# A routed two-layer feed-forward kernel: the blank bucket rows written last in the set-up, and the count of surely full tiles rounded up

## Chip, cores and metric

The kernel runs on one core of one Trainium2 chip. The metric is the device time of one launch in microseconds. It includes everything between the kernel's start and its last write: loading the weights, the scan, the routing, the matrix products and the scatter of the results.

## The reference

Two stages follow each other. The first is a gated recurrence along the sequence, for 4 batches of 5056 positions with 256 channels each. The second sends each of the 20224 resulting rows to the one expert of 8 with the largest logit, and applies that expert's two weight matrices (256 to 1024 to 256).

```python
sig = 1.0 / (1.0 + np.exp(-f_logit))
f = lower_bound + (1.0 - lower_bound) * sig
for t in range(S):
    h = f[:, t] * h + (1.0 - f[:, t]) * x[:, t]
    y[:, t] = h
...
logits = x @ w_gate
expert_idx = np.argmax(logits, axis=1)
gate_w = softmax(logits)[np.arange(N), expert_idx]
for e in range(E):
    mask = expert_idx == e
    h = np.maximum(x[mask] @ w1[e], 0.0)
    out[mask] = gate_w[mask, None] * (h @ w2[e])
```

## The kernel before

**Units.** The 20224 rows are worked on as 79 units of 256 rows. For each unit SP issues two loads (`load`, lines 248 and 249), ScalarE computes the gate (`prep`), VectorE runs the recurrence (`scan`, lines 264 to 277), and `split` scales the result, writes it as two fp16 halves and has SP transpose them into rows (line 297). `logits` multiplies by the gate matrix on TensorE (line 304).

**Groups and buckets.** Units are collected into 25 groups: one of 4 units, ten of 2, then groups of 4 (the last has 3). When a group's last unit is done, `route` finds each row's expert, and `place` works out where the row goes in that expert's bucket in DRAM (`idx`, line 352) and scatters the rows from GpSimd, 128 rows per indirect DMA (line 363). Bucket rows start 128 rows behind the bucket's first address. The first 128 rows of each bucket are written by `blank` (lines 238 to 243): a zeroed tile `zr`, whose token column lies out of bounds, is copied by one DMA of 8 x 128 rows of 1032 bytes. `zr` is taken from the rotation of three buffers with the tag `xT`.

**Tiles.** A tile is a run of 128 rows (groups 0 to 12) or 256 rows (groups 13 to 24) of one expert. Which expert has a full tile is known only on the chip, but how many tiles are surely full is known when the program is written: `guaranteed(n, size)` (line 57) gives it from the number n of rows that lie in the buckets and are not yet in a tile. `tile_info` (lines 380 to 428) then finds on VectorE the offset and the expert of that many tiles, in ten small instructions (lines 398 to 419), and puts the tiles into the list `todo`. What is left at the end goes into `NTAIL` tail tiles of 128 rows (`tail_info`); the last three of them stand in a branch that runs only if there are so many.

**Steps.** `prefetch` takes a tile of 256 rows, or two of 128 rows if the next in `todo` is one too, and has SP load it (`fetch`, lines 487 to 490): a register load of the offset, a transposing load of the rows into an `xT` buffer, and a small load `me`. At most three are fetched ahead. A `step` multiplies one fetched piece by w1 (`gemm1`, lines 508 to 510, three products for each pair of fp16 halves, in four blocks), evicts each block with ScalarE and VectorE (lines 513 and 514), and multiplies the piece of the step before by w2 (`gemm2`, lines 542 to 544, then line 548 and the scatter of line 549).

**Order.** The set-up follows the hand-written string `ORDER`. `L` loads one expert's weight matrix, `X` one unit, `P` runs `prep`, `T` finishes a unit up to its logits, `A`, `B`, `C` scale and split weights, `F` is `finish` (place the groups that are routed, and their tiles), `Q` is `prefetch`, `S` is a first step that holds only gemm1, and `W` is `blank`. In the set-up a scheduler may pull instructions forward in each engine's queue, but each engine works its queue in order. Behind the set-up TensorE, ScalarE and VectorE follow the program's own order: each step calls `fill` eight times if its gemm2 works on two tiles (four times in gemm1, twice for each tile of gemm2), and the parts of the next units are hung on these slots. The parts of a unit lie at fixed slots from its start: split at 0, scan of the next unit at 1, logits at 4, `finish` at 9. The distance to the next unit's start depends on the rows that are ready (in `todo` or fetched):

```python
def ready():
    return sum(t for t, _ in todo) + sum(f[4] for f in fetched)
...
plan_unit(tick(u), 5 if r < LOW else 6 if r < MID else 7 if r < HIGH else 8)
```

LOW, MID and HIGH are 1024, 1280 and 1792 rows.

Of the kernel before, what the change touches and what calls it, by code (L numbers as in the profile page):

```python
# [17 lines left out]
P = 128  # L18
D = 256
E = 8  # L20
F = 1024
# [16 lines left out]
LOW = 4 * UNIT  # L38
MID = 5 * UNIT
HIGH = 7 * UNIT  # L40
ORDER = "Q L X P X T Z L X L A0 P L X X L A1 W T B0 P X L L L P C0 T B1 T F P X Q A2 C1 Q P L A3 B2 L B3 C2 C3 L X T X T L L L F Z X L A4 B4 A6 T P P A5 X T C4 L P B5 B6 C5 C6 F A7 B7 T S Q C7"
EXPM = 0x7F800000
EVEN = 0x7F000000
MAGIC = 12582912.0
# [11 lines left out]

def guaranteed(n, size):

    return max(0, (n - E * (size - 1)) // size)


@with_exitstack
def moe_kernel(ctx: ExitStack, tc: tile.TileContext, x, fl, lb, wg, w1, w2, cst, tok, out, xb, S):
# [158 lines left out]
    def free(d, *groups, keep=()):  # L222

        for k in groups:
            tc.declare_no_dep(d.ins, group=k, keep=[s.ins for s in keep], reason="different rows")
# [10 lines left out]
    def blank():  # L236

        zr = p2.tile([P, ROW], F32, tag="xT", name="zr", bufs=3)
        nc.vector.memset(zr, 0.0)
        nc.vector.memset(zr.bitcast(I32)[:, D + 1:D + 2], OOB)  # L240
        d = nc.sync.dma_start(xb[0:E * CAP, :].rearrange("(e r) w -> r e w", e=E)[0:P], zr.unsqueeze(1).to_broadcast([P, E, ROW]))
        free(d, "scatter")
        tc.add_to_no_dep_group("blank", d.ins)

    def load(u):
# [312 lines left out]
    plan, n, taken = [], 0, 0  # L558
    while n < NU:
        gu = min(GROUPS[len(plan)] if len(plan) < len(GROUPS) else GRU, NU - n)  # L560
        n += gu
        size = P if len(plan) < SMALL else UNIT
        k = guaranteed(n * UNIT - taken, size)
        taken += k * size
        plan.append((gu, size, k))
# [128 lines left out]
    u = 0  # L694
    for w in ORDER.split():
        k, n = w[0], int(w[1:] or 0)
        if k == "L" and wl:
            wload(*wl.pop(0))
        elif k == "X":
            ahead(len(loaded))  # L700
        elif k == "P":
            preps(prepped[0])
        elif k == "Z":
            scans(scanned[0])
        elif k == "T":
            scans(u)
            t1 = tick(u)
            t1[2]()
            t1[3]()
            u += 1  # L710
        elif k == "A":
            stages[n] = wscale(*jobs[n][:2])
            stages[n][0]()
        elif k == "B":
            stages[n][1]()
        elif k == "C":
            stages[n][2]()
            jobs[n][2]()
        elif k == "W":
            blank()  # L720
        elif k == "F":
            finish()
        elif k == "Q":
            prefetch()
        elif k == "S":
            step(lambda k: None, False)
# [58 lines left out]
    if spare:  # L785
        n = nc.values_load(total[0])
# [93 lines left out]
```

## Time and profile before

| what | value |
|---|---|
| device time, median of 3 runs | 1008.66 us (1008.51 to 1011.13) |
| device time of the profiled execution | 1012.38 us |
| span of the profiled execution, first to last instruction | 1010.6 us |
| TensorE busy with products | 944.3 us (93%) |
| VectorE busy | 662.0 us (66%) |
| ScalarE busy | 485.4 us (48%) |
| GpSimd busy | 341.0 us (34%) |
| mean DMA rate | 144 GB/s |

The profile shows one execution. Shares over the whole span are averages over stages that differ: in the set-up the weights are loaded and split, behind it steps and units are interleaved, and at the end only steps are left. Such a profile is read by stages: first where TensorE, the busiest engine, stands idle, then what ended each idle stretch.

### The profile page before, as it was taken

The page shows a single profiled execution, that of the slowest core. Times are in us where ns is not written, and L with a number is a line of the kernel's source. Part 1 is how long each engine was busy: PE and PEld are TensorE (multiplying, and loading weights), DVE is VectorE, ACT ScalarE, POOL GpSimd, SP SyncE. Part 2 cuts the span into 40 slices and gives each one's busy share as a digit, 9 for nine tenths or more (in the row PEclk, how much of TensorE's full clock was granted, in tenths as well). Part 3 has the DMA queues.
Part 4 walks back from the last instruction along what each step waited for, and adds up shares of the span by engine and source line. Part 5 has one row for each costly group of instructions (what it writes and reads, how often), then busy time and mean ns, then how long its engine had stood idle before and what let it go on. Part 6 is the DMA issues. An engine that isn't in the chain of part 4 may idle for free.

```text
span 1010.6 us, 29046 instructions
## 1 busy us (share of the span) xinstructions
PE 944.3 (93%) x10815; PEld 852.6 (84%) x10815; DVE 662.0 (66%) x1885; ACT 485.4 (48%) x860; POOL 341.0 (34%) x351
## 2 busy tenths in 40 slices
PE   3549888999999999899999999999999999999998
PEld 3426877889999998888888888888888888899997
DVE  6987878778678677867877777677676423223231
ACT  4568544545545555545555555545553333233332
POOL 0141144434334533534552452442434321111212
PEclk9969988999999999999999999999999999999999
DMA  8997567979866767777786676567753321222211
GB/s 292 333 343 187 108 141 151 161 164 177 143 157 163 155 144 165 173 169 160 180 175 157 164 162 152 148 137 170 166 111 95 80 49 48 58 49 49 42 40 41
DMA packets 239579, 145.52 MB, mean 144 GB/s; under 512 B 205773, under 2 KB 207055, under 8 KB 237392
## 3 DMA queue, kind: packets, MB, share of 16 engines
q1 hardware_dynamic: 224080, 102.02, 47.8%
q0 software_dynamic: 15360, 41.60, 13.4%
q8 instruction: 92, 1.51, 0.6%
q14 instruction: 47, 0.39, 0.1%
HBM read 58.57 MB, written 43.16 MB: 101 GB/s over the span
## 4 chain that ended last, share of the span: by engine, by line
PE 57%; issue 17%; DMA 4%; POOL 4%; DVE 3%; ACT 1%; POOLq 1%; SPq 0%; DVEq 0%
PE g L508 9%; PE g L510 9%; PE g L509 9%; PE g L542 9%; PE g L544 9%; PE g L543 9%; POOL out_dram L549 3%; DMA out_dram<-ob,ti 3%; PE tp L304 1%; DMA buckets<-rows,idx 1%; DVE xt L274 1%; DVE hT L514 1%; POOL buckets L363 1%; PE tp L112 0%; DVE am L277 0%
## 5 line engine op out<-in xcount | busy, mean ns | idle before, releaser
L508 PE MATMUL g<-xT,w1s 128*128 128x128 f16 (+1 forms) x1904 | 401.7, 241 | 13.1 <-issue 5.9
L509 PE MATMUL g<-xT,w1s 128*128 128x128 f16 (+1 forms) x1904 | 401.4, 241 | 0.0
L510 PE MATMUL g<-xT,w1s 128*128 128x128 f16 (+1 forms) x1904 | 401.4, 241 | 0.0
L514 DVE SCALAR_TENSOR_TENSOR hT<-g,hT 128x512 f16<-128x512 f32 x324 | 219.1, 686 | 220.9 <-ACT hT L513 217.4
L542 PE MATMUL g<-w2s,hT 128*128 x1296 | 353.6, 273 | 0.3 <-issue 0.3
L544 PE MATMUL g<-w2s,hT 128*128 x1296 | 353.8, 273 | 0.0
L543 PE MATMUL g<-w2s,hT 128*128 x1296 | 353.7, 273 | 0.0
L549 POOL DMA_INDIRECT out_dram<-ob,me x142 | 147.4, 1038 | 375.8 <-ACT ob L548 305.5
L513 ACT ACTIVATE hT<-g 128x512 f16<-128x512 f32 x324 | 188.8, 592 | 164.4 <-PE g L510 160.8
L363 POOL DMA_INDIRECT buckets<-rows,idx x158 | 166.5, 1054 | 194.1 <-issue 115.3
L508 PEld LDWEIGHTS <-w1s 128*128 x1904 | 188.5, 99 | 22.1 <-issue 10.4
L509 PEld LDWEIGHTS <-w1s 128*128 x1904 | 188.7, 99 | 10.2 <-issue 2.3
L510 PEld LDWEIGHTS <-w1s 128*128 x1904 | 188.7, 99 | 8.2
L548 ACT ACTIVATE ob<-g,fac 128x256 f32<-128x256 f32 x162 | 76.1, 471 | 187.1 <-PE g L544 180.0
L544 PEld LDWEIGHTS <-hT 128*128 128x128 f16 x1296 | 126.9, 98 | 14.9
L543 PEld LDWEIGHTS <-hT 128*128 128x128 f16 x1296 | 126.8, 98 | 14.3 <-issue 0.6
L542 PEld LDWEIGHTS <-hT 128*128 128x128 f16 x1296 | 126.8, 98 | 14.0
L274 DVE TENSOR_TENSOR_SCAN xt<-ft,xt,xt 128x256 f32<-128x256 f32 (+2 forms) x156 | 110.1, 730 | 1.2
L295 DVE SCALAR_TENSOR_TENSOR ft<-xt,m,ft 128x256 f16<-128x256 f32 x158 | 72.2, 481 | 56.6 <-ACT ft L292 52.6
L292 ACT ACTIVATE ft<-xt,m 128x512 f16<-128x512 f32 x79 | 56.9, 721 | 74.8 <-DVE m L289 71.7
L257 ACT ACTIVATE ft<-ft,fa,fs 128x256 f32<-128x256 f32 x158 | 86.4, 593 | 2.4
L255 ACT ACTIVATE ft<-ft 128x512 f32<-128x512 f32 x79 | 49.3, 623 | 20.4 <-DMA ft<-in_f 18.2
(129 smaller groups left out, 613.5 us busy)
## 6 DMA issues: line engine op xcount, KB each, us to landing
ft<-in_f SPq DMA_DIRECT2D x79, 256.0 KB
xt<-in_x SPq DMA_DIRECT2D x79, 256.0 KB
w2s<-in_w SPq DMA_DIRECT2D x14, 1024.0 KB
rows<-ft SPq DMA_TRANSPOSE x158
buckets<-rows,idx POOLq DMA_INDIRECT x158
out_dram<-ob,me POOLq DMA_INDIRECT x142
ws<-in_w SPq DMA_DIRECT2D x2, 1024.0 KB
xT<-buckets SPq DMA_TRANSPOSE x122
```

Source lines behind the costliest of these rows:

```text
L257: nc.scalar.activation(ft[:, c, :], ft[:, c, :], AF.Identity, scale=fs[:, c:c + 1], bias=fa[:, c:c + 1])
L274: nc.vector.tensor_tensor_scan(xt[:, c, a:b], ft[:, c, a:b], xt[:, c, a:b], ini, op0=ALU.mult, op1=ALU.subtract)
L363: d = nc.gpsimd.indirect_dma_start(out=xb[:, :], out_offset=bass.IndirectOffsetOnAxis(ap=idx[:, i:i + 1], axis=0), in_=rows[:, i, 0:ROW], ...
L508: nc.tensor.matmul(o, lhsT=hi, rhs=xT[:, c, a:a + nt], start=c == 0, stop=False)
L509: nc.tensor.matmul(o, lhsT=hi, rhs=xT[:, 2 + c, a:a + nt], start=False, stop=False)
L510: nc.tensor.matmul(o, lhsT=lo, rhs=xT[:, c, a:a + nt], start=False, stop=c == 1)
L513: nc.scalar.activation(hh, ps[:, :, :n], AF.Relu)
L514: nc.vector.scalar_tensor_tensor(hT[:, 1, 2 * b:2 * b + 2, :n], ps[:, :, :n], 0.0, hh, op0=ALU.max, op1=ALU.subtract)
L542: nc.tensor.matmul(po[:, :D], lhsT=hh, rhs=hi, start=f == 0, stop=False)
L543: nc.tensor.matmul(po[:, :D], lhsT=hh, rhs=lo, start=False, stop=False)
L544: nc.tensor.matmul(po[:, :D], lhsT=hl, rhs=hi, start=False, stop=f == NF - 1)
L549: d = nc.gpsimd.indirect_dma_start(out=out[:, :], out_offset=bass.IndirectOffsetOnAxis(ap=ti[j], axis=0), in_=ob, in_offset=None, bounds_c ...
```

## The change

`W` moves from the place behind `A1` to the end of `ORDER`, so `blank` is now called behind the first step `S`. Since loads of tiles now stand ahead of it in the program, its DMA is also declared free of those loads. And `guaranteed` rounds its quotient up instead of down.

```diff
-ORDER = "... L X X L A1 W T B0 P X ... A7 B7 T S Q C7"
+ORDER = "... L X X L A1 T B0 P X ... A7 B7 T S Q C7 W"
...
 def guaranteed(n, size):
 
-    return max(0, (n - E * (size - 1)) // size)
+    return max(0, -((E * (size - 1) - n) // size))
...
     def blank():
...
-        free(d, "scatter")
+        free(d, "scatter", "load")
```

## Rows read from the trace of the kernel before

**Rows 1.** The page's first line, its line of TensorE and VectorE with busy time, share and instructions, and the 40 slices of the span for TensorE (tenths busy) and for its granted clock (tenths of full speed).

```profile
span 1010.6 us, 29046 instructions
PE 944.3 (93%) x10815; PEld 852.6 (84%) x10815; DVE 662.0 (66%) x1885; ACT 485.4 (48%) x860; POOL 341.0 (34%) x351
...
PE   3549888999999999899999999999999999999998
...
PEclk9969988999999999999999999999999999999999
```

**Rows 2.** Busy time of each engine in six stretches of the span, with granted clock, DMA share and rate.

```profile
0.00:95.40 95.40, 54.37 (x421) 36.70 (x421) 75.48 (x212) 58.55 (x73) 16.81 (x21) 0.91 0.98 300
95.40:224.80 129.40, 114.99 (x1539) 107.23 (x1540) 102.53 (x341) 65.48 (x122) 48.09 (x50) 0.93 0.70 142
224.80:392.30 167.50, 165.51 (x2353) 155.92 (x2351) 127.15 (x370) 88.34 (x164) 67.62 (x70) 1.00 0.77 159
392.30:442.90 50.60, 46.82 (x603) 42.41 (x602) 38.33 (x107) 25.89 (x49) 17.15 (x18) 0.97 0.72 157
442.90:778.90 336.00, 335.88 (x3362) 301.81 (x3360) 246.73 (x682) 175.67 (x325) 140.99 (x141) 1.00 0.68 155
778.90:1010.60 231.70, 226.70 (x2546) 208.48 (x2544) 71.80 (x178) 71.50 (x129) 50.30 (x51) 0.99 0.22 51
```

**Rows 3.** The two largest waits of TensorE between 95.4 and 224.8 us: total, times, longest.

```profile
PE tp L112 <- DVE am L277: 5.8, 3, 2.1
PE g L508 <- issue: 5.5, 3, 2.1
```

**Rows 4.** TensorE in order of time around 430 us: the first product of a step with the idle time ahead of it, two products at their later distance, and the first instruction behind that step's second block.

```profile
430.14 0.28 PE L508 MATMUL g<-xT,w1s 128*128 128x256 f16 x1 [2.45 <-DMA xT<-buckets]
...
431.02 0.42 PE L509 MATMUL g<-xT,w1s 128*128 128x256 f16 x1
431.23 0.42 PE L510 MATMUL g<-xT,w1s 128*128 128x256 f16 x1
...
434.44 0.22 PE L112 MATMUL tp<-half,am 128*128 128x128 bf16 x1
```

**Rows 5.** What feeds the product at 430.14 us: VectorE's instruction that gives the addresses, the first and last of GpSimd's eight scatters, and three pieces of the chain that ended last.

```profile
409.54 0.21 DVE L352 TENSOR_REDUCE idx<-sh 128x8 int32<-128x64 f32 x1
```

```profile
412.05 1.31 POOL L363 DMA_INDIRECT buckets<-rows,idx  x1 [6.69 <-issue]
...
421.89 0.96 POOL L363 DMA_INDIRECT buckets<-rows,idx  x1 [0.31 <-issue]
```

```profile
421.89 5.03 DMA buckets<-rows,idx
...
426.98 3.11 DMA xT<-buckets
```

**Rows 6.** Groups of the page by line: a third of the products of gemm1, and the evictions of gemm1 by VectorE.

```profile
L508 PE MATMUL g<-xT,w1s 128*128 128x128 f16 (+1 forms) x1904 | 401.7, 241 | 13.1 <-issue 5.9
...
L514 DVE SCALAR_TENSOR_TENSOR hT<-g,hT 128x512 f16<-128x512 f32 x324 | 219.1, 686 | 220.9 <-ACT hT L513 217.4
```

**Rows 7.** TensorE in order of time at the first steps: the first product of `S`, its last one, the first of the next step, and two later starts with the idle time ahead of them.

```profile
95.49 0.22 PE L508 MATMUL g<-xT,w1s 128*128 128x128 f16 x1 [0.22 <-ACT w2s L211]
...
100.79 0.22 PE L510 MATMUL g<-xT,w1s 128*128 128x128 f16 x1
101.50 0.22 PE L508 MATMUL g<-xT,w1s 128*128 128x128 f16 x1 [0.49 <-DVE hT L514]
...
129.48 0.23 PE L112 MATMUL tp<-half,am 128*128 128x128 bf16 x1 [2.08 <-DVE am L277]
...
131.58 0.29 PE L508 MATMUL g<-xT,w1s 128*128 128x128 f16 x1 [1.87 <-issue]
```

**Rows 8.** A stretch of 2 us behind that last start, as in rows 2.

```profile
132.00:134.00 2.00, 2.00 (x21) 2.00 (x20) 1.39 (x7) 0.23 (x1) 1.40 (x2) 0.50 0.57 81
```

**Rows 9.** VectorE in order of time: the two instructions that fill `zr` and one that fills a count for group 1, an idle stretch in the set-up, and the last split of w2.

```profile
1.04 0.27 DVE L239 MEMSET zr<- 128x258 f32 x1
1.27 0.07 DVE L388 MEMSET kk<- 128x8 f32 x1
...
50.48 0.42 DVE L178 TENSOR_REDUCE wam<-wps 128x2 f32<-128x256 f32 x1 [1.38 <-PE wps L175]
...
102.56 2.34 DVE L203 SCALAR_TENSOR_TENSOR w2s<-ws,wsc,w2s 128x2048 f16<-128x2048 f32 x1
```

**Rows 10.** Two of the ten groups of `tile_info` on VectorE, one of the cheapest and the dearest.

```profile
L413 DVE TENSOR_TENSOR pr<-mk,val 128x96 f32<-128x96 f32 (+3 forms) x23 | 5.7, 250 | 0.1
...
L404 DVE TENSOR_TENSOR val<-start,pin 128x8 f32<-128x8 f32 x23 | 3.5, 151 | 0.0
```

**Rows 11.** SP's queue in the set-up: the blank rows' DMA, and later two transposes and a weight load around 60 us.

```profile
22.77 0.43 SPq L241 DMA_DIRECT2D buckets<-zr  x1
...
59.38 2.51 SPq L297 DMA_TRANSPOSE rows<-ft  x2
61.99 0.53 SPq L153 DMA_DIRECT2D w2s<-in_w  x1
```

**Rows 12.** The first and the last of the eight scatters of group 0 on GpSimd.

```profile
46.48 1.32 POOL L363 DMA_INDIRECT buckets<-rows,idx  x1 [42.45 <-DVE idx L352]
...
57.72 2.07 POOL L363 DMA_INDIRECT buckets<-rows,idx  x1 [0.30 <-issue]
```

More of the change, by code (lines that the diff above doesn't have):

```diff
@@ L40 @@
 HIGH = 7 * UNIT
-ORDER = "Q L X P X T Z L X L A0 P L X X L A1 W T B0 P X L L L P C0 T B1 T F P X Q A2 C1 Q P L A3 B2 L B3 C2 C3 L X T X T L L L F Z X L A4 B4 A6 T P P A5 X T C4 L P B5 B6 C5 C6 F A7 B7 T S Q C7"
+ORDER = "Q L X P X T Z L X L A0 P L X X L A1 T B0 P X L L L P C0 T B1 T F P X Q A2 C1 Q P L A3 B2 L B3 C2 C3 L X T X T L L L F Z X L A4 B4 A6 T P P A5 X T C4 L P B5 B6 C5 C6 F A7 B7 T S Q C7 W"
 EXPM = 0x7F800000
```

## The prediction

> **What bounds the kernel now.** I read the page's first part and its slices first [rows 1], then the busy time by stages [rows 2], then, for each stage in which TensorE is idle, its waits and the instructions around them [rows 3 to 8]. TensorE is busy for 944.3 of 1010.6 us, so only 66.3 us can be won without taking products away. By stages: 41.0 us of that lie in the set-up (95.4 less 54.4), 14.4 us between 95.4 and 224.8, 2.0 us up to 392.3, 3.8 us between 392.3 and 442.9, nearly nothing for the next 336 us, and 5.0 us at the end. Busy time hides one more loss: a product at half clock counts as busy. So I also compare the time of a step. Counting the gemm1 products of line 508 in order of time (32 for each step of two 128-row tiles, 16 for a 256-row tile) puts step 29 at 442.9 and step 60 at 778.9, so a step costs 336.0 / 31 = 10.84 us when nothing is wrong. The stretch from 392.3 holds steps 25 to 28: 50.6 / 4 = 12.65 us each, 7.2 us too much in all. From 101.5 to 224.8 lie steps 1 to 9: 13.7 us each, 25.8 us too much [rows 2, 7].
>
> **What the change does to the schedule.** I worked this out from the code, by following ORDER, the drips and the planner by hand.
>
> Rounding up: group 0 has 1024 rows, and (1024 - 8 x 127) / 128 = 8 / 128 becomes 1 surely full tile, not 0. All other groups keep their counts (4, 8 or 4 tiles), so 143 instead of 142 units of 128 rows are sure, and the tail has 22 slots instead of 23. The tail's real tiles drop by exactly one, so the final branch is taken or not as before. TensorE's products are unchanged: the 1904 of line 508 stay 1904 [rows 6]. What changes is their place. The lone tile of group 0 becomes the first step, so `S` holds 48 gemm1 products instead of 96; the tail has 19 tiles in front of the branch, so its last step is a lone tile too. There are 82 steps instead of 81, and from the second step on there are 128 rows more in reserve. The planner sees them: units 9 and 10 start 6 slots apart, not 5, and unit 25 starts at slot 95 instead of 91.
>
> **Set-up.** `tile_info` of group 0 now runs there: ten VectorE instructions of 0.15 to 0.25 us [rows 10], together 1.8 us by their own groups' means, an upper bound since those means come from 3 to 8 tiles and this is one. They come behind `place` of group 0, near 46 us, and VectorE idles 1.38 us soon after, waiting for TensorE [rows 9]. That cover leaves 0.4 us; without it the cost is 1.8. I take +0.5.
>
> The fetch of that tile (one transposing load, one `me` load, one register load on SP) is moved ahead of loads in SP's queue, and may run only when all eight scatters of group 0 have landed. The last one starts at 57.72 [rows 12]; at the 5.03 us that another scatter took to land, that is 62.8 [rows 5]. SP works in order: whatever stands behind the fetch waits. Around that time SP waits for transposes anyway and issues a weight load at 61.99 [rows 11], so if the fetch stands where its data are expected the cost is about 0 to 1 us. It is the second rival otherwise.
>
> The blank DMA: 8 x 128 x 1032 bytes = 1.06 MB. At the 300 GB/s of the set-up that is 3.5 us of DMA time [rows 2]. It leaves the loads' way at 22.77 us [rows 11], but VectorE is busy for 75.5 of the 95.4 us and nearly always from 20 to 50 us, so loads that land earlier mostly wait. Nor is the place in ORDER the place in the queue: `zr` is filled at 1.04 us and a count that belongs to group 1 at 1.27 us [rows 9], both far ahead of their place in the list. The DMA may be pulled forward into any gap of SP's queue. `zr` then holds one of the three `xT` buffers longer. Bounds: a gain of 3.5 us, a loss of as much if it lands in the way of the last weights. I take 0.
>
> **First steps.** `S` took 5.3 us for 96 products (95.49 to 100.79) and now takes 2.7; the next gemm1 ends near 95.5 + 2.7 + 5.3 = 103.5 instead of 106.9, but w2's last split on VectorE starts at 102.56 and takes 2.34, so gemm2 waits up to 1.4 us [rows 7, 9]. VectorE has less to evict by then, so I take +0.5. From there to 224.8 TensorE waits in turn for VectorE: 5.8 us for the scan's maximum, 5.5 us at starts of steps [rows 3]. VectorE's work for units 9 to 25 is unchanged, and TensorE gets four more slots of its own work in between: 4 x 10.84 / 8 = 5.4 us, less the 2.7 us that `S` no longer does, less one wider gap's evictions, at most 4 x 0.69 / 2 = 1.4 us [rows 6]. That is 1.3 us; I take -1, with bounds of -5 (a fifth of the 25.8 us) and +3.5.
>
> **The switch to 256-row tiles.** Group 13 yields no tile, so the reserve runs low before group 14 delivers the first tile of 256 rows. Before, group 14's `finish` is at slot 198 and its first tile is needed at slot 216: 18 slots. After, at 201 and 222: 21 slots, since a step more is in front. The path in between: addresses at 409.54, eight scatters from 412.05 to 421.89, 5.03 us to land, 3.11 us for the transposing load [rows 5]. TensorE waited 2.45 us for it at 430.14, and then ran at half clock: products of 256 columns 0.21 us apart at 431.2, and 24 of them took 4.3 us to 434.44, where 2.7 us are due at twice the 0.056 us that lie between products of 128 columns (95 distances from 95.49 to 100.79) [rows 4, 7]. Three slots more are 3 x 1.34 = 4.0 us, which covers the 2.45. Then nothing lets the clock fall. Gain: 2.45 + 1.6 = 4.05 us, at most the 7.2 us of the stretch, at least 0. What is late next there are the scans, which the planner still packs at 5 slots (four units instead of three); I take -4.
>
> The Trainium skill (TensorE: Matmul & The Clock Gate, What's actually happening) states that the throttled clock is the default and that activity releases it. The trace agrees: 0.50 granted behind an idle stretch at 132 us. By that rule the shorter `S` speaks against the change, too.
>
> **End.** One step more: 0 to 2 us, the size of a start's issue wait [rows 7]; I take +0.3. The path behind the last product is the same.
>
> **Sum.** +0.5 + 0 + 0.5 - 1 - 4 + 0.3 = -3.7 us. Against the profiled execution: 1010.6 - 3.7 = 1006.9 us of span, 1.8 us lie around it, so 1008.7 instead of 1012.4. The median is 1008.66, 0.4% below the profiled execution, so it becomes 1004.9 us. A measurement of this kernel tells about 0.3% (3 us) from no change.
>
> **Rivals.**
> First: the wait moves. The gain at the switch comes, but a new gap opens behind the short `S`: 2 us of waiting and 2 us at half clock, as around 129.5 to 136 us (idle 2.08 and 1.87, then 21 products in 2 us where 36 fit) [rows 7, 8]. Sum about 0: 1008.5 us. For it: VectorE is the late engine there; against it: the next gemm1 is ready.
> Second, slower: SP stands still at group 0's fetch. If it is queued ahead of the loads that follow 50 us, SP holds them until 62.8 us; weights reach TensorE up to 10 us later, of which the 41 us idle of the set-up hide part. At 8 us the sum is +4: 1013 us. It decides from a stall of 7 us on. For it: the queue's order is fixed before the run, and real landings are late here; against it: SP loses time to transposes already. The Trainium skill (Perfetto Trace Analysis, Sequencer Loop) describes each engine's sequencer as taking one instruction after the other; the trace's weight load right behind the transposes fits that.
> Third, more gain: the blank DMA's 3.5 us come off the set-up and the first steps lose a fifth of their loss: 1000 us.
> Fourth: the extra reserve is there, but the switch is late all the same, since the scatters and the fetch wait on other queues: gain under 2 us, 1007.5 us.
>
> **How the numbers follow.** Chances: forecast 0.45 (its own spread 1001.5 to 1007), first rival 0.17, second 0.13, third 0.15, fourth 0.10. Faster by over 0.3% means below 1005.6: the third, and about four fifths of the forecast: 0.51. Slower means over 1011.7: 0.12. The rest, 0.37, lies within. The range reaches from 998 (below the third rival) to 1011, leaving out the second rival's upper part.
>
> **What would show it.** Right: `S` with 48 products, no wait for `xT` near 427 us and a granted clock of 1.00 there, steps 25 to 28 near 11.3 us, a first product near 96 us. Wrong: a set-up beyond 100 us with SP waiting for bucket scatters near 55 us; a half-clock stretch right behind `S`; TensorE still waiting for `xT` at the switch.

## The result, and the profile after

The kernel after the change takes 1025.26 us in the median of four runs (1021.48 to 1026.51), the kernel before beside it 1009.83 us in the median of four. The ratio is 1.0147, with an interval of 1.0113 to 1.018: slower, where the forecast was 1004.9 us. The profiled execution of the kernel after took 1021.48 us with a span of 1019.7 us, so the span grew by 9.1 us. The profiled execution of the kernel before (1012.38 us) is longer than its median, and that of the kernel after is the shortest of its four, so the two traces hold only 9.1 of the 15.4 us between the medians. In the third group of experiments below, two of the twenty executions of the kernel before took over 5300 us, and its median and the ratios there leave them out.

The page of the kernel after: span, two engines, and three rows of the 40 slices (TensorE, granted clock, GB/s).

```profile
span 1019.7 us, 29061 instructions
PE 941.0 (92%) x10815; PEld 847.9 (83%) x10815; DVE 667.3 (65%) x1901; ACT 487.9 (48%) x864; POOL 341.4 (33%) x351
...
PE   3617888999999999899999999999999999999998
...
PEclk9967999999999999999999999999999999999999
...
GB/s 290 321 157 293 94 199 141 173 166 150 162 144 152 159 149 180 173 161 181 148 189 155 161 144 169 153 163 148 148 112 106 79 59 55 50 53 46 42 41 40
```

TensorE has the same 10815 products and is busy 3.3 us less than before [rows 1], although the span is longer: the loss is idle time. The slices say where. The third slice, 51 to 76 us, has 1 where it had 4, and there the DMA engines fall to 157 GB/s. From the fifth slice on the two kernels look alike. So the set-up comes first.

Busy time of the kernel after in stretches (us, then busy time of PE, PEld, DVE, ACT and POOL with counts, granted clock, DMA share, GB/s).

```profile
0.00:95.40 95.40, 43.63 (x367) 32.28 (x367) 69.31 (x212) 47.38 (x61) 18.96 (x21) 0.84 0.88 271
...
55.00:60.00 5.00, 0.66 (x4) 0.56 (x4) 5.00 (x5) 2.68 (x3) 4.39 (x3) 0.65 0.16 55
60.00:65.00 5.00, 0.51 (x6) 0.32 (x6) 2.11 (x6) 0.00 (x0) 1.74 (x2) 0.50 0.15 54
65.00:70.00 5.00, 0.00 (x0) 0.00 (x0) 0.00 (x0) 0.00 (x0) 0.00 (x0) 0.50 0.78 245
70.00:75.00 5.00, 0.11 (x1) 0.11 (x2) 1.55 (x5) 1.72 (x3) 0.00 (x0) 0.50 1.16 272
75.00:80.00 5.00, 1.49 (x15) 0.76 (x14) 5.00 (x29) 1.31 (x3) 1.02 (x2) 0.50 0.97 367
80.00:85.00 5.00, 2.91 (x13) 1.41 (x14) 4.76 (x18) 4.91 (x6) 3.73 (x4) 0.50 0.99 358
85.00:90.00 5.00, 5.00 (x65) 4.86 (x64) 3.42 (x9) 1.95 (x4) 0.00 (x0) 0.78 1.16 377
90.00:95.00 5.00, 4.34 (x28) 2.46 (x27) 4.25 (x17) 3.07 (x7) 0.00 (x0) 1.00 1.20 225
```

Between 65 and 70 us no engine works, and for ten microseconds before that the DMA engines carry some 55 GB/s. All engines are short of input at once, so whoever issues the loads has stopped. That is SP; its queue in order of time (start, duration):

```profile
43.15 0.38 SPq L153 DMA_DIRECT2D w2s<-in_w  x1
63.62 1.22 SPq L488 DMA_TRANSPOSE xT<-buckets  x1
65.06 0.39 SPq L490 DMA_DIRECT2D me<-buckets  x1
65.58 0.35 SPq L153 DMA_DIRECT2D w2s<-in_w  x1
66.02 0.38 SPq L248 DMA_DIRECT2D ft<-in_f  x1
...
91.02 0.41 SPq L153 DMA_DIRECT2D ws<-in_w  x1
```

For 20.1 us, from 43.5 to 63.62, SP issues nothing. What it stands at is the fetch of the new lone tile, line 488. Its waits between 40 and 107 us, and those that follow from them on ScalarE, VectorE and TensorE (total, times, longest):

```profile
SPq L488 <- DMA buckets<-rows,idx: 11.0, 4, 4.9
SPq L487 <- DVE ii L419: 8.0, 1, 8.0
```

```profile
ACT ft L255 <- DMA ft<-in_f: 16.6, 2, 14.0
```

```profile
DVE xt L264 <- ACT ft L257: 11.9, 2, 11.3
```

```profile
PE tp L112 <- DVE am L277: 14.4, 2, 14.0
```

First SP waits 8.0 us to load the register with the tile's offset (`ii`, line 419, which VectorE writes at 51.35), then 11.0 us for group 0's scatters. The unit's load behind it comes 14.0 us late for ScalarE, and each engine passes the delay on. The chain of work that ended last shows the same, read downwards:

```profile
57.77 2.89 POOL buckets L363
...
60.97 2.57 DMA buckets<-rows,idx
63.62 1.22 SPq L488
...
66.02 5.55 DMA ft<-in_f
71.66 0.64 ACT ft L255
```

The first gemm1 product starts at 106.66 us instead of 95.49 [rows 7], 11.2 us later. To follow that loss I give, for each kernel, the time at which a given row starts in gemm1. It is found by counting the products of line 508 in order of time; where a row lies inside a step, it is placed in proportion between the step's start and the next.

| row | before | after | difference |
|---|---|---|---|
| 0 (first product) | 95.5 | 106.7 | +11.2 |
| 2560 | 224.8 | 231.3 | +6.5 |
| 6400 (ahead of the switch to 256-row tiles) | 392.3 | 400.0 | +7.7 |
| 7424 | 442.9 | 449.5 | +6.6 |
| 9216 | 519.1 | 528.1 | +9.0 |
| 20224 (the last tiles) | 979.0 | 988.1 | +9.1 |

So the set-up loses 11.2 us, the first steps give back 4.7, the steps up to row 6400 lose 1.2, the stretch around the switch gives back 1.1, and the steps right behind the switch lose 2.4. From row 9216 on the two kernels take the same time.

TensorE of the kernel after around the switch, the counterpart of [rows 4]:

```profile
429.14 0.23 PE L112 MATMUL tp<-half,am 128*128 128x128 bf16 x1 [0.99 <-DVE am L277]
431.45 0.23 PE L508 MATMUL g<-xT,w1s 128*128 128x128 f16 x1 [2.08 <-issue]
```

The wait of 2.45 us for `xT` is gone. A wait of 0.99 us for the scan's maximum and one of 2.08 us ahead of a step's first product stand ahead of a step of 128-row tiles, and the granted clock between 430 and 435 us is 0.69 on average. The wait has moved. The 2.08 us are TensorE's register work for the step's two experts, which stands in its queue behind the waiting product: two register loads (line 497) and the register instructions that follow them, up to the product at 431.45. The loads:

```profile
L497 PEldq TENSOR_LOAD <-ii x2: 319/568/817, 429.1 to 429.8; - x2
```

The columns are durations in ns (least, median, longest) and the first and last start.

### The profile page after: what moved, and what is told of

Same layout as the page of the kernel before. It is cut to its first block, busy times and chain, and to the rows that moved or that the text cites. A ratio compares the mean times of both kernels' runs of the same rounds, so it can differ in the third digit from the quotient of the medians.

```text
span 1019.7 us, 29061 instructions
## 1 busy us (share of the span) xinstructions
PE 941.0 (92%) x10815; PEld 847.9 (83%) x10815; DVE 667.3 (65%) x1901; ACT 487.9 (48%) x864; POOL 341.4 (33%) x351
## 3 DMA queue, kind: packets, MB, share of 16 engines
q8 instruction: 92, 1.51, 0.6%
## 4 chain that ended last, share of the span: by engine, by line
PE 55%; issue 17%; DVE 13%; DMA 6%; POOL 4%; ACT 3%; SPq 1%; POOLq 0%; DVEq 0%; ACTq 0%
PE g L508 9%; PE g L510 9%; PE g L542 9%; PE g L509 9%; PE g L544 9%; PE g L543 9%; POOL out_dram L549 3%; DMA out_dram<-ob,ti 3%; DVE xt L274 2%; DVE hT L514 2%; DMA ft<-in_f 2%; DVE ft L295 2%; DVE am L277 1%; DVE xt L264 1%; ACT ft L292 1%
## 5 line engine op out<-in xcount | busy, mean ns | idle before, releaser
L508 PE MATMUL g<-xT,w1s 128*128 128x128 f16 (+1 forms) x1904 | 397.6, 239 | 11.3 <-issue 4.6
L510 PE MATMUL g<-xT,w1s 128*128 128x128 f16 (+1 forms) x1904 | 397.4, 239 | 0.0
L509 PE MATMUL g<-xT,w1s 128*128 128x128 f16 (+1 forms) x1904 | 397.4, 239 | 0.0
L514 DVE SCALAR_TENSOR_TENSOR hT<-g,hT 128x512 f16<-128x512 f32 (+1 forms) x328 | 220.9, 681 | 224.3 <-ACT hT L513 222.8
L513 ACT ACTIVATE hT<-g 128x512 f16<-128x512 f32 (+1 forms) x328 | 190.5, 587 | 165.0 <-PE g L510 162.4
L363 POOL DMA_INDIRECT buckets<-rows,idx x158 | 166.7, 1055 | 194.3 <-issue 94.9
```

The costliest lines, as they stand in the source:

```text
L363: d = nc.gpsimd.indirect_dma_start(out=xb[:, :], out_offset=bass.IndirectOffsetOnAxis(ap=idx[:, i:i + 1], axis=0), in_=rows[:, i, 0:ROW], ...
L508: nc.tensor.matmul(o, lhsT=hi, rhs=xT[:, c, a:a + nt], start=c == 0, stop=False)
L509: nc.tensor.matmul(o, lhsT=hi, rhs=xT[:, 2 + c, a:a + nt], start=False, stop=False)
L510: nc.tensor.matmul(o, lhsT=lo, rhs=xT[:, c, a:a + nt], start=False, stop=c == 1)
L513: nc.scalar.activation(hh, ps[:, :, :n], AF.Relu)
L514: nc.vector.scalar_tensor_tensor(hT[:, 1, 2 * b:2 * b + 2, :n], ps[:, :, :n], 0.0, hh, op0=ALU.max, op1=ALU.subtract)
```

## Experiments

Runs in one group shared a chip and the runs of the kernel before.

**First group: take the change apart.** The theory after the result was that the early fetch stops SP. The rivals were that the blank DMA or the tile's ten small VectorE instructions cost the time, or that the different schedule behind the set-up does.

*The blank rows last, rounding down as before.*

```diff
-... A1 W T B0 ... S Q C7
+... A1 T B0 ... S Q C7 W
-        free(d, "scatter")
+        free(d, "scatter", "load")
```

> The blank rows are written last, as in the change, but the number of sure tiles is rounded down, as before. Theory (SP's queue: the fetch of group 0's tile stands ahead of weight loads and holds them until group 0's scatters have landed): no such fetch here, so the first gemm1 product comes at 92 to 97 us and the time is 1004 to 1011 us, the kernel before's. Rival A (the moved blank DMA and the buffer that its tile holds are what costs): 1015 to 1026 us, with the first product near 95 us and the loss behind it. Rival B (the rounding's new schedule costs by itself: the lone tile's step, the ten VectorE instructions, the other unit distances): 1008 to 1011 us.

Measured: 1009.48 us beside 1007.99, ratio 1.0004 [0.9987, 1.0022]; first product at 94.9 us. This half of the change costs and brings nothing that can be measured.

*Rounding up alone, the blank rows at their old place.*

```diff
-    return max(0, (n - E * (size - 1)) // size)
+    return max(0, -((E * (size - 1) - n) // size))
```

> The sure tiles are rounded up, as in the change, but the blank rows are written where they were before. Theory (SP's queue): the fetch of group 0's tile still stands ahead of the weight loads, SP does nothing between about 43 and 63 us, the first gemm1 product comes at 104 to 110 us, and the time is 1017 to 1028 us. Rival A (blank): about 1010 us. Rival B (schedule): 1015 to 1026 us, but with the first product before 99 us.

Measured: 1022.09 us, ratio 1.0111 [1.0076, 1.0146]; first product at 107.8 us. SP's queue of this kernel has the same hole:

```profile
46.00 0.33 SPq L248 DMA_DIRECT2D ft<-in_f  x1
63.22 1.22 SPq L488 DMA_TRANSPOSE xT<-buckets  x1
```

The loss belongs to the rounding.

*The whole change, but the lone tile is fetched late.* The two early calls of `prefetch` are taken out of the set-up's list, and the first tile is kept alone:

```diff
-... T F P X Q A2 C1 Q P L A3 ...
+... T F P X A2 C1 P L A3 ...
-            if tiles[0][0] == P and todo and todo[0][0] == P:
+            if nst and tiles[0][0] == P and todo and todo[0][0] == P:
```

> The changed kernel, but the two calls of prefetch early in the list are taken out, so the lone tile of group 0 is fetched only in the first step, with the next two pieces; that it stays alone in its piece is written out. Theory (SP's queue): weight loads no longer stand behind that fetch, the first gemm1 product comes at 93 to 98 us, and the time is 1002 to 1012 us, so nearly all of the loss is gone. Rival A (blank) and rival B (schedule): both are unchanged here, so 1018 to 1026 us.

Measured: 1014.07 us, ratio 1.0043 [1.0016, 1.007]; first product at 95.6 us, as before the change. `tile_info`, the extra step and the rounded schedule are all still there, so none of them delays the set-up. What is left, 0.4%, comes later.

*The kernel before, with one small read in SP's queue.* At the same place SP reads two columns of a bucket, a read that has to wait for group 0's scatters and that nobody uses:

```diff
+            if scatters and not probes:
+                pb = sm.tile([P, 2], F32, tag="pb", name="pb", bufs=1)
+                d = nc.sync.dma_start(pb, xb[P:2 * P, D:D + 2])
+                guard(d, len(scatters), None)
+                probes.append(d)
```

> The kernel before (rounded down, blank rows early), with one small DMA more: at the place of the first early prefetch behind group 0's scatters, SP reads 128 rows x 2 words of the buckets into a tile that nothing uses, and waits for those scatters as a fetch does. Theory (SP's queue): the wait alone makes the loss: SP stands still until about 63 us, the first gemm1 product comes at 103 to 110 us, and the time is 1015 to 1027 us. Rivals A and B: nothing of theirs is in this kernel, so 1008 to 1012 us.

Measured: 1014.08 us, ratio 1.0064 [1.004, 1.0088]; first product at 100.4 us. SP issues nothing between 46.03 and 62.26. Both the time and the first product lie below what the theory expected: the wait alone costs, but only part of what the change costs.

**Second group: the rest of the loss, on a chip where it can't be read.** The theory on the 2.4 us behind the switch: the rounding puts 128 rows more in reserve, and the distance of two units goes by that reserve. By hand, the distances of units 39 to 47 are 6 5 5 5 7 6 6 5 7 before and 6 5 5 5 5 7 6 5 5 after; scans are packed closer, and VectorE is late for TensorE. Three edits go with it: the planner reads 128 rows less (in the late fetch), the planner never goes below 6 slots (in the kernel before), and, against the other wait seen at the switch, the registers of the next step are loaded in the middle of the step before (in both kernels).

```diff
+        p = r - P
-            plan_unit(tick(u), 5 if r < LOW else 6 if r < MID else 7 if r < HIGH else 8)
+            plan_unit(tick(u), 5 if p < LOW else 6 if p < MID else 7 if p < HIGH else 8)
```

```diff
-            plan_unit(tick(u), 5 if r < LOW else 6 if r < MID else 7 if r < HIGH else 8)
+            plan_unit(tick(u), 6 if r < MID else 7 if r < HIGH else 8)
```

```diff
+        if fetched and not early:
+            regs[fetched[0][0]] = experts(fetched[0][1])
...
-        evs = [nc.tensor.value_load(i[1], min_val=0, max_val=(E - 1) * WE) for _, i in tiles]
+        evs = regs.pop(t, None) or experts(tiles)
```

The late fetch with 128 rows less, and the kernel before with at least 6 slots:

> The late-fetch kernel (blank rows last, sure tiles rounded up, group 0's tile fetched only in the first step), and the planner sees 128 rows fewer than are ready, so the unit distances around units 39 to 47 are the ones of before again (6 5 5 5 7 6 6 5 7 instead of 6 5 5 5 5 7 6 5 5). Theory (what was left of the loss behind the set-up is the planner's: the rows in reserve shift the moments at which it looks, and two units in a row are packed 5 slots apart once more): the stretch from row 7424 to row 9216, 78.6 us in the three kernels that round up and 76.2 us in the others, is 76.2 to 76.8 us here; the time is 1006 to 1011 us. Rival (the lone tile and the shifted pairs cost by themselves): the stretch stays at 78.6 us and the time at 1010 to 1016 us.

> The kernel before, with units never closer than 6 slots (they were 5 apart for 12 units). Theory (VectorE sets the pace where units are 5 slots apart, and TensorE waits for it): TensorE's idle time between 95 and 225 us falls from 14.4 us to under 10, and the time is 1000 to 1007 us. Rival (the rows would run out: fewer units in time, so TensorE waits for tiles instead): the waits move to tiles loaded from the buckets, and the time is 1008 to 1016 us.

The early registers, in the kernel before and in the late fetch:

> The kernel before, with TensorE's register loads of a step's experts issued a half step earlier, between gemm1 and gemm2 of the step in front. Theory (the idle time of about 2 us that the trace puts to no releaser at the start of a step is two register loads in a row that stand behind a product which waits for VectorE, so they cannot run ahead): the idle time without releaser ahead of line 508, 5.9 us in four places, falls under 2 us, and the time falls by 3 to 8 us, to 1000 to 1006 us. Rival (these idle times are something else, such as the fetching of instructions): they stay, and the time is 1007 to 1011 us.

> The late-fetch kernel with the register loads moved in the same way. Theory: at the switch to 256-row tiles no 2 us idle time is left, so steps 26 to 28 take under 36 us together (after: 38.3 us), and the time is 1004 to 1010 us. Rival: 1010 to 1016 us, as the late-fetch kernel without it.

Measured, in this order: 0.9972 [0.994, 1.0004], 1.0076 [1.0041, 1.0111], 1.0112 [1.0063, 1.016] and 1.0115 [1.0081, 1.0149]. But the kernel before itself took 1146.65 us on this chip, 14% more than elsewhere, so differences of a few microseconds can't be carried over from there. What is special shows in TensorE's largest waits, here of the first of the four:

```profile
PE g L508 <- issue: 19.6, 25, 1.9
PE g L509 <- issue: 16.0, 27, 1.1
...
PE g L510 <- issue: 13.6, 22, 1.8
```

Waits that nothing in the profile ends are spread over lines 508 to 510, where the page of the kernel after has 4.6 us of them at line 508 and no idle time at 509 and 510. Their cause stays open. The fetching of instructions, named as a rival above, doesn't show as slower in the transfers, which doesn't rule it out: the page's row of the queue of kind `instruction` is the same as in the kernel before (92 packets, 1.51 MB, 0.6%). The planner with 128 rows less and the early registers in the kernel before were run again elsewhere. The planner that never goes below 6 slots and the early registers in the late fetch were not, so what they would do on another chip stays open.

**Third group: is the fetch enough by itself, and the rest once more.** First, the kernel before with a whole fetch as a dummy at that place: register load, transposing load and small load, unused.

```diff
+                off = nc.sync.value_load(tk[0:1, 1:2], min_val=0, max_val=E * CAP)
+                d = nc.sync.dma_start_transpose(px, xb16[ds(off, P), 0:2 * D])
+                guard(d, len(scatters), None)
+                d = nc.sync.dma_start(pb, xb[ds(off, P), D:D + 2])
+                guard(d, len(scatters), None)
```

> The kernel before, with a whole fetch in the place of the probe's small read: a register load, a transposing load of 128 bucket rows into a tile that nothing uses, and the small load, both waiting for group 0's scatters. The probe moved the first gemm1 product from 95.5 to 100.4 us, the change to 106.7. Theory (the fetch itself in SP's queue makes the whole delay of the set-up, the transposing load's own time included): first product at 103 to 109 us, time 7 to 13 us above the kernel before. Rival (a wait in SP's queue costs about 5 us, and the rest comes from the new order of VectorE's work in the set-up when it meets this wait): first product at 99 to 102 us, time 4 to 7 us above.

Measured: 1020.43 us beside 1008.27, ratio 1.0117 [1.0086, 1.0147]; first product at 106.9 us. SP's queue and two stretches near the end of the set-up:

```profile
46.66 0.34 SPq L153 DMA_DIRECT2D w2s<-in_w  x1
60.02 1.23 SPq L729 DMA_TRANSPOSE px<-buckets  x1
61.48 0.38 SPq L731 DMA_DIRECT2D pb<-buckets  x1
61.91 0.90 SPq L153 DMA_DIRECT2D w2s<-in_w  x2
```

```profile
85.00:90.00 5.00, 5.00 (x57) 5.00 (x54) 3.39 (x15) 0.83 (x3) 0.00 (x0) 0.60 1.19 286
90.00:95.00 5.00, 2.83 (x15) 1.55 (x14) 4.51 (x17) 4.23 (x5) 0.00 (x0) 0.74 1.34 347
```

A fetch whose result nobody uses, in a kernel that is otherwise the one before, delays the set-up as the change does (11.4 us against 11.2). That is enough to settle the main cause, the early fetch in SP's queue. That the two delays agree to 0.2 us is in part luck: the dummy's hold lasts 13.0 us and makes the last load into `ws` 8.9 us late, the change's lasts 20.1 us and makes it 10.7 us late. How the small read comes to cost less is partly visible. In all four kernels with a hold the last load into `ws` is 7.9 to 11.6 us late:

| kernel | SP issues nothing | 12th load into `w2s` | last load into `ws` | first product |
|---|---|---|---|---|
| before | - | 62.0 | 80.35 | 95.5 |
| after | 43.5 to 63.6 | 73.1 | 91.02 | 106.7 |
| rounding alone | 46.3 to 63.2 | 74.6 | 91.95 | 107.8 |
| dummy fetch | 47.0 to 60.0 | 71.6 | 89.28 | 106.9 |
| small read | 46.0 to 62.3 | 70.2 | 88.24 | 100.4 |
| late fetch | - | 55.0 | 79.58 | 95.6 |

The dummy fetch's last load is 1.0 us behind the small read's, its first product 6.5 us. In the same two stretches the kernel with the small read has a granted clock of 1.00, the one with the dummy fetch 0.60 and 0.74, as shown. The price of the half clock, 1.2 GHz, can be read from the same eight products of line 209, first with the small read, then with the dummy fetch:

```profile
88.79 3.70 PE L209 MATMUL lo<-w2s,dg 128*128 128x512 f32 x8 [1.32 <-DVE dg L206]
```

```profile
93.27 6.64 PE L209 MATMUL lo<-w2s,dg 128*128 128x512 f32 x8 [0.72 <-DVE dg L206]
```

That is 2.9 of the 6.5 us. The rest is not separated: the order of the loads and of TensorE's products differs too.

*The late fetch again.* The kernel of the first group, on this chip.

> The late-fetch kernel once more, beside the next one on the same chip. Theory (the planner's distances cost 2 to 3 us, the chip's spread the rest): ratio to the kernel before 1.001 to 1.006.

Measured: 1014.46 us, ratio 1.0065 [1.0045, 1.0086].

*The late fetch with 128 rows less, again.*

> [...] Theory (planner): the stretch from row 7424 to row 9216 is 76.2 to 76.8 us, ratio to the kernel before 0.996 to 1.001. Rival (lone tile and shifted pairs): stretch 78.6 us, ratio 1.002 to 1.007.

Measured: 1012.0 us, ratio 1.0039 [1.0015, 1.0062]. The stretch from row 7424 to row 9216, first of the kernel after, then of this one:

```profile
449.50:528.10 78.60, 76.73 (x774) 68.51 (x773) 63.22 (x175) 43.24 (x80) 34.33 (x35) 1.00 0.81 169
```

```profile
439.90:516.00 76.10, 76.10 (x773) 68.46 (x771) 60.59 (x172) 41.53 (x78) 39.50 (x39) 1.00 0.84 186
```

It takes 78.6 or 78.7 us in the kernel after, with the rounding alone and in both runs of the late fetch, and 76.1 to 76.3 us in the kernel before, with the blank rows last, with either dummy, and here. The planner's distances explain these 2.4 us. The two medians of this group differ by as much (1014.46 and 1012.0), but the intervals of their ratios overlap, so it is the stretch that shows it. By the program, the planner is not the one of before everywhere: the distances behind units 18 and 19 are 5 and 5 here, 6 and 7 in the kernel before. And the ratio stays above 1, in the range of the rival, so this is not all of the rest.

*The kernel before with early registers, again.*

> [...] Theory (two register loads behind a waiting product are the 2 us idle times at a step's start): the idle time without releaser ahead of line 508 falls from 5.9 us to under 2 us, ratio to the kernel before 0.992 to 0.997. Rival: 0.998 to 1.012, with the loads' wait moved into the middle of the step.

Measured: 1026.46 us, ratio 1.017 [1.013, 1.0209]. The time is beyond the rival's range too. The wait ahead of gemm1 is gone, and larger ones stand ahead of gemm2's first line, 547 in this kernel and 542 before:

```profile
PE g L547 <- ACT hT L518: 15.9, 22, 1.0
...
PE g L547 <- issue: 9.6, 13, 1.0
```

The likely reading is that most of the register loads run beside other work at the old place, where waits without a releaser ahead of line 508 come to 5.9 us in four places, and that many don't at the new one. The loss of 2 us at a step's start is not won back this way.

## Why the prediction was wrong

**Set-up: the step that failed.** I put the fetch of the lone tile at "about 0 to 1 us", "if the fetch stands where its data are expected", and the sum holds nothing for it. It stands 20.1 us ahead of its data. The second rival named the mechanism and the place (SP holds the loads until 62.8 us; measured 63.6), but I gave it 0.13. The argument "SP loses time to transposes already" was true but not enough: between 43.5 and 63.6 us the kernel before issues at least five weight loads, six loads for units and four transposes. The kernel after issues two of these weight loads ahead of the hold (at 42.10 and 43.15) and nothing in it. Behind the hold the queue caught up a part, from the 11th weight load to the 12th in 7.6 us (65.58 to 73.14), where the kernel before needs over 12 (its 11th is issued by 49.49, its 12th at 61.99). So of 20.1 us of standing 11.2 were left at the first product. The Trainium skill (DMA: Bandwidth & Descriptors, Anatomy of one DMA — SWDGE (gpsimd) path) says of DMA engines in general that a transfer's wait is done by the engine that issues it, ahead of the issue, and not by them; the trace agrees, with no transfer issued by SP for 20.1 us while other loads were due. The rival's 8 us was too small: the weights' last load is 10.7 us late, and the set-up's idle time hid none of it. Both halves of this could be read beforehand: in the list `Q` stands three letters behind the first `F`, and the eight scatters for which it waits run from 46.48 to 57.72 us [rows 12]. I had the second and didn't lay the first beside it.

**`tile_info`, +0.5.** Not contradicted: with the late fetch the instructions still run and the first product is at 95.6 us. But they had a second effect that I left out: SP's register load waits 8.0 us for their last result. It is covered here, since the scatters hold SP longer anyway.

**Blank rows, 0.** The time was right (1.0004), the reason was not. I took the early fill of a count as a sign that the fill of `zr` would be pulled forward too. In the trace of after the fill and the DMA stand late, since `zr` takes its turn in the rotation of the `xT` buffers:

```profile
L239 DVE MEMSET zr<- x1: 273/273/273, 116.9 to 116.9; 128x258 f32 x1
```

```profile
L241 SPq DMA_DIRECT2D buckets<-zr x1: 433/433/433, 126.1 to 126.1; - x1
```

**First steps, +0.5 - 1.** The sign was right. From row 0 to row 2560 the kernel before takes 129.4 us, the kernel after 124.7. With the rounding it takes 122.7 to 126.1 us in four executions, with the old rounding 126.4 to 130.8 in four, and 127.1 with the rounding but 128 rows less for the planner. So the reserve probably helps here, by the planner's distances, but the two ranges nearly touch (126.1 and 126.4), and how much it brings stays open. It isn't just the set-up's loss regained: with the dummy fetch the set-up is as late and the stretch takes 130.8 us.

Against it works the gap that the first rival named, behind the short `S`. With the rounding alone, in both late fetches and with 128 rows less, TensorE waits 3.2 us behind `S` for VectorE's evictions, where it waits 1.1 us in the kernel after and at most 0.8 us in the kernels that round down (the early registers left out). In the late fetch of the first group, VectorE first splits w2, then evicts the four blocks of `S`, and TensorE waits for that:

```profile
99.00 2.34 DVE L203 SCALAR_TENSOR_TENSOR w2s<-ws,wsc,w2s 128x2048 f16<-128x2048 f32 x1
...
101.25 1.41 DVE L514 SCALAR_TENSOR_TENSOR hT<-g,hT 128x256 f16<-128x256 f32 x4
```

```profile
101.73 0.26 PE L508 MATMUL g<-xT,w1s 128*128 128x128 f16 x1 [3.24 <-DVE hT L514]
```

```profile
101.00:105.00 4.00, 3.27 (x32) 3.27 (x32) 3.92 (x6) 1.48 (x3) 2.13 (x2) 0.50 0.19 66
```

The last row shows the granted clock at 0.50 behind the wait. In the kernel before the same split runs from 98.51 to 100.85 us, the 96 products of `S` last as long, and a wait of 0.49 us is left [rows 7].

**The switch, -4.** The wait of 2.45 us for `xT` is gone, as forecast. But of the 4.05 us only 1.1 came, and even these hang on the one execution of the kernel before. The three other kernels that round down (blank rows last, small read, dummy fetch) wait 1.5 to 2.0 us for `xT` there, keep a granted clock of 1.00 and take 48.2 to 48.6 us; the four that round up with the full reserve take 49.0 to 50.4 us at 0.97. So no gain is shown here. That is the first rival's mechanism, a wait that moves, at another place: what was late next were the scans, as I had written, and I gave that no price. Behind a 0.99 us wait came 2.08 us of register work, and then half clock. With 128 rows less for the planner, so that the distances around the switch are those of before, the wait for `xT` and the one of 2.08 us are both gone, the wait for the scan's maximum is 0.6 us as in the kernel before, and the stretch takes 46.1 us at a clock of 1.00, in the one execution profiled in the third group:

```profile
393.80:439.90 46.10, 44.54 (x594) 40.89 (x593) 37.83 (x111) 26.18 (x50) 16.96 (x17) 1.00 0.79 170
```

That is 4.4 us less than in the profiled execution of the kernel before, near the 4.05 us that I had reckoned, and 2.1 to 2.5 us less than in the other three that round down. What this term left out is that the extra rows also change the distances of the units.

**What no step had.** The reserve of 128 rows also acts through the planner: +2.4 us behind the switch, with the distances as the cause (78.6 against 76.1 us). I had followed the units only to number 25. A second loss lies ahead of the switch. From row 2560 to row 6400 the five executions that round up, outside the second group (the planner with 128 rows less among them, with 169.9 us), take 168.7 to 171.0 us, and TensorE is idle for 2.8 to 4.9 us of it; the four that round down, the early registers left out, take 167.3 to 167.7 us, with 1.7 to 2.1 us idle. Since it stands with 128 rows less too, the reserve that the planner sees doesn't explain it. The lone tile and the shifted pairs are the rival that is left; no run tests them alone.

**The sum.** In the profiled executions: +11.2 - 4.7 + 1.2 - 1.1 + 2.4 + 0.1 = +9.1 us. The terms behind the set-up lean on the execution set beside them: the kernel with only the blank rows moved rounds down as the kernel before does and has a span of 1006.7 us, and beside it the first steps give back 1.8 us and the switch loses 1.0. The last 0.1 us lies behind row 9216, where I had taken +0.3 for the end. By medians the change costs 1.5%, some 15 us; the dummy fetch alone costs 1.2%, the rounding with a late fetch 0.4 to 0.65%. Of that rest 2.4 us are the distances. With these taken off, 0.39% [0.15%, 0.62%] is left, some 4 us. Some 2 us of it can be the loss between rows 2560 and 6400; its cause and the remainder stay open. The spans can't settle it: the profiled executions of the third group with a late fetch have 1009.3 and 1007.3 us and are among the shortest of their kernels, while the 1010.6 us of the kernel before are among its longest. None of the versions beats the kernel before.

## What to carry to other kernels

A transfer that waits for late data is cheap only if nothing behind it in the same queue is needed sooner: before moving one forward, list what that queue would issue until the data land. A change of a count that a planner reads (here rows in reserve) moves work far from the place of the edit, so follow its decisions through to the end of the program. A wait that disappears is worth only its distance to the next one.

## What was not expected of the hardware

Two register loads in a row on TensorE's own queue, 0.30 us each in the median of a hundred, made a gap of 2.08 us where they stood behind a waiting product: the loads took 0.32 and 0.82 us, and the register instructions behind them most of the rest. With the loads moved into the middle of a step the kernel is 1.7% slower.

The granted clock stays at 0.50 through the recovery: from 60 to 85 us TensorE is at its lower level, 1.2 GHz, in the kernel after, though it has products again from 74.9 us on, and the clock rises in the stretch from 85 us, which is filled without a gap (0.78, then 1.00). The Trainium skill (TensorE: Matmul & The Clock Gate, What's actually happening) describes that order, slow by default and released by activity, and the trace agrees.

One chip ran the kernel before 14% slower and the four kernels tried there about as much, with idle time ahead of matrix products that nothing in the profile ends.
